# The product with w_spatial as seven products of quarters, whose forms of w_spatial are kept in HBM

## The chip, the core and the metric

The kernel runs on one core of a Trainium2 chip. The metric is device time in microseconds (us), the median of several executions. A core has TensorE (PE in the profile; PEld is its weight load), VectorE (DVE), ScalarE (ACT) and GpSimd (POOL) for the arithmetic, and SyncE (SP), whose queue issues all the DMAs here. Matmuls read their two operands from SBUF and add up in banks of PSUM; the other engines bring results from there back to SBUF.

## What is computed

```python
def _attn_ref(q, k, v, n_global, n_local):          # 4 batches, 8 heads, 768 tokens, head_dim 64
    scores = scale * np.matmul(q, k.transpose(0, 1, 3, 2))
    keep = is_global | is_local                      # 8 global keys, 96 local ones
    scores = np.where(keep, scores + bias, -1000000000.0)
    a = np.exp(scores - max)
    a = a / (sum + 1e-09)
    return np.matmul(a, v)

def _moe_ref(x, w_in, w_spatial, b_spatial, w_out):  # x: [4, 768, 512], w_in: [512, 1024]
    h = np.maximum(x @ w_in, 0.0)
    u, v = (h[..., :d_ff // 2], h[..., d_ff // 2:])
    v_n = (v - mu) / np.sqrt(var + 1e-06)            # mean and variance over the 512 features
    v_s = np.einsum('ts,bsd->btd', w_spatial, v_n) + b_spatial[None, :, None]
    return (u * v_s) @ w_out                         # w_spatial: [768, 768], w_out: [512, 512]
```

The einsum is the product that the change is about: for each batch a 768 x 768 matrix times 768 tokens x 512 features.

## The kernel before

A batch has 768 tokens, six blocks of 128. The program walks through 24 blocks, n = 0 to 23, of attention (scores S, exponentials, transposes, values A), and between them does the pieces of the second function, named by letters in the table `CFG`: V (relu and normalization of one block's v), U (the relu of u for a chunk of 256 tokens), G (the product with w_spatial for a chunk, and the gate), O (the product with w_out, and the result's DMA), and in the first batch the loads: I (w_in), Q (w_out), T (w_spatial), B (b_spatial). The digit behind the letter is the lag in batches, the next the chunk or block: G and O of a batch run while the attention of the next batch does; for the last batch they stand in `END`, with nothing of a next batch beside them.

To keep float32 accuracy, an operand is held as two numbers of TensorE's fast float32 format, a rounded one and the rest (`hi_lo`: a copy that rounds, and a subtraction), and each product is three passes: high by high, high by low, low by high. In `mlp_s` (G) a chunk takes, for each of four blocks of 128 features, 3 passes x 6 blocks of source tokens, that is 18 matmuls of 128x128 by 128x256. Over 3 chunks and 4 batches that is 864 matmuls. The weights' side, `w_t_h` and `w_t_l`, is loaded and split once (`setup_w_t`) and stays in SBUF; the normalized v is split per block into `vnh` and `vnl` (`mlp_v`). Of two accumulated results DVE adds b_spatial (`ev<-bank,b_bc`), DVE or POOL multiplies by u, and `hi_lo` makes `gh` and `gl`, which `mlp_o` multiplies by w_out.

The calls between on and off of the recorder are not issued but recorded, and a planner (`plan`) then sets the order on every engine: it plays the program through with a table of costs (`cost`), waits between engines (`CROSS`) and ranks (`RANKS`, one number for each recorded operation), and picks an engine where an operation may run on several (`any_of`, fixed by `PINS`). PSUM is handed out as six banks by the same planner. `keep_warm` puts matmuls that nobody reads (transposes of the identity, fillers below) into stretches of the start where the planner sees TensorE without work for over 0.9 us. The order is fixed in the program; on the chip every engine works through its own list, and waits where an operand isn't there.

## Time and profile before

| what | value |
|---|---|
| median of 3 runs | 466.04 us (465.19 to 467.04) |
| the profiled execution's own time | 465.66 us |
| its span, first to last instruction | 463.8 us |
| TensorE busy | 449.2 us, 97% |
| VectorE / ScalarE / GpSimd busy | 299.8 / 205.1 / 194.3 us |
| bytes moved by DMA | 35.97 MB, 78 GB/s on the mean |
| granted TensorE clock, mean | 0.992 of full speed |

The busy times say how full an engine is on the mean; what sets the end is in the chain of waits, which follows the last instruction back to what released it, piece by piece. A busy TensorE isn't one at its peak: the time from one matmul's start to the next one's is read from its timeline.

### The profile page before, as it was taken

To read this page: it belongs to the slowest core of one execution; us is meant where nothing else is said; L and a number is where in the kernel's file an instruction comes from. 1 tells how busy PE (TensorE), PEld (TensorE's weight loads), DVE (VectorE), ACT (ScalarE), POOL (GpSimd) and SP (SyncE) were. 2 spreads that over 40 slices of the span, in tenths; PEclk is the share of its full clock that TensorE was granted. 3 is DMA by queue.
4 is the path that set the end of the run, shared out by engine and by line. 5 is a ranking of instruction groups with operands and counts; after the bars stand their busy time and mean duration, and the time that the engine had idled before them with its cause. 6 is when DMAs were issued, how large, how long until landed. Compare 5 with 4: busy or idle time off the path is not lost.

```text
span 463.8 us, 9906 instructions
## 1 busy us (share of the span) xinstructions
PE 449.2 (97%) x3712; PEld 402.2 (87%) x3712; DVE 299.8 (65%) x922; ACT 205.1 (44%) x593; POOL 194.3 (42%) x295
## 2 busy tenths in 40 slices
PE   8579999999999999999999999999999999999996
PEld 8457789899888989899988989899989889899995
DVE  4889998925677899854146898885332577742333
ACT  3877875310448676532012687565011454610001
POOL 2988564334357545221323745365013436211311
PEclk9889999999999999999999999999999999999999
DMA  7876123300213223201012323120002011000012
GB/s 259 309 250 213 61 78 116 116 24 10 105 47 114 98 76 101 92 2 47 1 45 75 114 96 99 52 93 25 1 24 74 24 52 53 7 1 1 23 47 75
DMA packets 17531, 35.97 MB, mean 78 GB/s; under 512 B 2116, under 2 KB 2372, under 8 KB 17476
## 3 DMA queue, kind: packets, MB, share of 16 engines
q1 hardware_dynamic: 17476, 35.27, 23.2%
q8 instruction: 31, 0.51, 0.5%
q14 instruction: 24, 0.20, 0.1%
HBM read 28.97 MB, written 6.29 MB: 76 GB/s over the span
## 4 chain that ended last, share of the span: by engine, by line
PE 90%; DVE 4%; DMA 3%; issue 1%; SPq 0%; POOL 0%; ACT 0%; DVEq 0%
PE bank L49 73%; PE ops L47 8%; PE bank L47 8%; DMA u<-in_moe_w_in_dram 2%; DVE pr L49 1%; DMA vring<-in_v_dram 1%; DVE bank L49 1%; DVE w_in_l L49 1%; SPq L49 0%; POOL pr L49 0%; DVE rawh L49 0%; DVE xtl L49 0%; DVE q L49 0%; DVE rc L49 0%; DVE ev L49 0%
## 5 line engine op out<-in xcount | busy, mean ns | idle before, releaser
L49 ACT ACTIVATE pr<-pr,mn 128x256 f32<-128x256 f32 (+1 forms) x192 | 92.2, 483 | 18.8 <-DVE mn L49 17.2
L49 DVE CUSTOM_DVE_ANT_0 pr<-bank,bias 128x256 f32<-128x256 f32 (+1 forms) x192 | 69.8, 395 | 24.8 <-PE bank L49 14.0
L49 POOL TENSOR_SCALAR pr<-pr,rc 128x256 f32<-128x256 f32 (+1 forms) x115 | 55.5, 495 | 53.6 <-DVE rc L49 26.1
L49 ACT ACTIVATE ev<-bank 128x512 f32<-128x512 f32 (+1 forms) x37 | 21.6, 584 | 97.0 <-PE bank L49 92.0
L49 PE MATMUL bank<-ident,pr 128*128 128x128 f32 x352 | 54.3, 279 | 7.6 <-POOL pr L49 5.9
L49 DVE TENSOR_TENSOR ev<-bank,b_bc 128x512 f32<-128x512 f32 x24 | 16.6, 690 | 59.4 <-PE bank L49 54.0
L49 PEld LDWEIGHTS bank<-ident,pr 128*128 128x128 f32 x352 | 40.9, 142 | 15.5 <-POOL pr L49 6.9
L49 ACT ACTIVATE pth<-bank 128x512 f32<-128x512 f32 (+1 forms) x67 | 36.2, 560 | 37.2 <-PE bank L49 33.7
L47 PE MATMUL ops<-pth,vring 128*64 128x128 f32 x704 | 44.5, 279 | 0.0
L47 PE MATMUL bank<-kring,q 64*128 64x256 f32 (+1 forms) x528 | 43.6, 307 | 0.7 <-DVE mn L49 0.7
L49 PE MATMUL bank<-w_t_l,vnh 128*128 128x256 f32 x288 | 44.2, 282 | 0.0
L47 PEld LDWEIGHTS ops<-pth,vring 128*64 128x64 f32 x704 | 38.7, 139 | 5.7 <-issue 4.3
L49 PE MATMUL bank<-w_t_h,vnh 128*128 128x256 f32 x288 | 42.9, 282 | 0.0
L49 PE MATMUL bank<-w_t_h,vnl 128*128 128x256 f32 x288 | 42.8, 282 | 0.0
L47 PEld LDWEIGHTS bank<-kring,q 64*128 64x128 f32 x528 | 35.0, 188 | 8.2 <-issue 3.7
L49 POOL TENSOR_TENSOR gl<-ev,gh 128x512 fp32r<-128x512 f32 x14 | 18.1, 1293 | 53.3 <-PE bank L49 34.7
L49 PEld LDWEIGHTS bank<-w_t_l,vnh 128*128 128x128 f32 x288 | 39.0, 189 | 0.7
L49 PEld LDWEIGHTS bank<-w_t_h,vnh 128*128 128x128 f32 x288 | 38.1, 189 | 0.5 <-issue 0.2
L49 PEld LDWEIGHTS bank<-w_t_h,vnl 128*128 128x128 f32 x288 | 38.0, 189 | 0.5 <-issue 0.2
L49 ACT ACTIVATION_READ_ACCUMULATOR pr<-pr,mn 128x1 f32 x192 | 36.4, 189 | 0.0
L49 PE MATMUL bank<-xth,w_in_l 128*128 128x256 f32 x192 | 33.7, 287 | 0.0
L49 DVE TENSOR_SCALAR pr<-pr,rc 128x256 f32<-128x256 f32 (+1 forms) x77 | 32.2, 443 | 0.5
(133 smaller groups left out, 870.9 us busy)
## 6 DMA issues: line engine op xcount, KB each, us to landing
vring<-in_v_dram SPq DMA_DIRECT2D x24, 256.0 KB, 2.8
out_dram<-ev SPq DMA_DIRECT2D x23, 256.0 KB, 2.0
u<-in_moe_w_in_dram SPq DMA_DIRECT2D x8, 512.0 KB, 5.1
rawh<-in_q_dram SPq DMA_DIRECT2D x9, 256.0 KB, 2.5
raw<-in_q_dram SPq DMA_DIRECT2D x9, 256.0 KB, 2.7
raw<-in_k_dram SPq DMA_DIRECT2D x9, 256.0 KB, 2.6
rawh<-in_k_dram SPq DMA_DIRECT2D x9, 256.0 KB, 2.8
kring<-in_k_dram SPq DMA_DIRECT2D x6, 256.0 KB, 5.0
```

Source lines behind the costliest of these rows:

```text
L47: self.real.matmul(**{n: placed(x) for n, x in kw.items()})
L49: getattr(self.real, self.call)(*[placed(x) for x in self.args], **{n: placed(x) for n, x in self.kw.items()})
```

## The change

The 768 x 768 matrix is cut into four quarters of 384 x 384, and v into four quarters of 384 tokens x 256 features (even or odd token blocks, lower or upper features). The result's quarters are then built from seven products of quarters, where a plain product takes eight. Each product takes sums or differences of quarters on both sides:

- `setup_w_t` makes the seven forms of w_spatial (four additions of 384 columns per pair of token blocks), `put_t` splits each with `hi_lo` and stores it to HBM: 3 pairs x 7 forms, 21 stores of 393 KB. Before, six blocks were split into SBUF.
- `mlp_s` (G, now seven steps per batch, in the order 0, 1, 4, 3, 6, 5, 2) loads one form, 1.18 MB, into one of two buffers `wts`: 28 loads, 33.0 MB. It makes v's side (`sx`, four additions of 128x768 per batch), splits it (`oper`), and does 2 x 9 matmuls of 128x128 by 128x384: 126 per batch, 504 in all. Each of the two results is added from PSUM by DVE (`ga`, `gt`, `gx`, each 128x384), joined with others in SBUF, and multiplied into u in place (`gate`).
- `mlp_v` no longer splits v; it stays whole for the batch (`vr`, one buffer). u is one tile for the batch (one buffer). `mlp_o` (O, six steps of 128 tokens) splits the gated u into `gg` right before its matmuls; their number and shape stay.
- The tables `RANKS` and `PINS` are new, and the entries of `CFG`: T moves from the first three to the fourth to sixth block of the first batch, Q into the second batch (`T1`). w_in's loads take the same slots as before (three parts of the tile `u`); the path for wide masks follows the new `mlp_s` and `mlp_o`, and isn't run with these inputs.

```diff
@@ -25,11 +25,12 @@
...
 CFG = {
     "WS": 6, "conv": "pp", "SG": 4, "SG0": 2, "WG": 4, "kept": "p", "bias1": "x", "bias2": "x", "whi": "x", "wth": "x", "wtl": "x",
-    "qhi": "x", "qlo": "x", "khi": "x", "klo": "x", "pth": "x", "xh": "x", "xl": "v", "vnh": "x", "vnl": "x",
+    "qhi": "x", "qlo": "x", "khi": "x", "klo": "x", "pth": "x", "xh": "x", "xl": "v", "wts": "x", "oph": "x", "opl": "x", "ops": "x", "gk": "x", "b_ga": 2, "b_gd": 2, "b_gt": 2, "b_gx": 3, "b_gx2": 2, "b_oper": 2, "b_wts": 2,
     "gm": "x", "gh": "x", "gl": "x", "o": "vava", "norm0": "x", "norm": "x", "vrn": "v", "b_ev": 3, "b_pr": 10, "b_pth": 4,
-    "S": [["I01", "A"], ["I00", "T00", "T01", "A", "V00", "B00"], ["T02", "T03", "A", "V01", "U00"], ["T04", "T05", "A", "V02"], ["Q00", "Q01", "A", "V03", "U01"], ["Q02", "Q03", "A", "V04"]],
-    "T": [["V15", "U12", "A"], ["G10", "O10", "A"], ["G11", "O11", "A"], ["G12", "O12", "V00", "V01", "U00", "A"], ["V02", "A"], ["V03", "U01", "A", "V04"]],
-    "END": ["V05", "U02", "G00", "O00", "G01", "O01", "G02", "O02"],
+    "S": [["I01", "A"], ["I00", "A", "V00", "B00"], ["A", "V01", "U00"], ["T00", "A", "V02"], ["T01", "A", "V03", "U01"], ["T02", "A", "V04"]],
+    "T1": [["V15", "U12", "A"], ["Q00", "Q01", "G10", "G11", "G12", "A"], ["Q02", "Q03", "G13", "G14", "G15", "A"], ["G16", "O10", "O11", "V00", "V01", "U00", "A"], ["O12", "O13", "V02", "A"], ["V03", "O14", "O15", "U01", "A", "V04"]],
+    "T": [["V15", "U12", "A"], ["G10", "G11", "G12", "A"], ["G13", "G14", "G15", "A"], ["G16", "O10", "O11", "V00", "V01", "U00", "A"], ["O12", "O13", "V02", "A"], ["V03", "O14", "O15", "U01", "A", "V04"]],
+    "END": ["V05", "U02", "G00", "G01", "G02", "G03", "G04", "G05", "O03", "G06", "O04", "O05", "O00", "O01", "O02"],
 }
 NLMAX = 97
...
-WORDS = {"gh": 1024, "gl": 1024, "pth": 512, "vring": 1536, "kring": 2048, "pr": 256, "s": 512, "p": 512, "m": 512, "ops": 1024, "q0": 1024, "q1": 1024}
-BUFS = {"gh": 1, "gl": 1, "u": 3, "s": 2, "p": 2, "m": 2, "raw0": 1, "raw1": 1, "rawh0": 1, "rawh1": 1}
+WORDS = {"gg": 1024, "oper": 1536, "u": 3072, "wts": 2304, "gx2": 768, "pth": 512, "vring": 1536, "kring": 2048, "pr": 256, "s": 512, "p": 512, "m": 512, "ops": 1024, "q0": 1024, "q1": 1024}
+BUFS = {"u": 1, "gg": 2, "s": 2, "p": 2, "m": 2, "raw0": 1, "raw1": 1, "rawh0": 1, "rawh1": 1}
...
 RANKS = [
-    -1227.13, -1206.24, -272.31, -662.83, 46.11, -326.88, -663.12, -104.90, -322.98, 496.15, -312.43, -1165.63, -37.37, -80.04, -1204.73, -1162.10,
+    -410.76, -386.18, -131.71, -256.51, -115.72, -216.04, -217.17, -54.52, -50.49, 10.95, -223.60, -450.53, -4.15, -17.85, 95.48, 0.39,
...
@@ -961,9 +950,11 @@
...
-    w_t_h = const.tile([P, NB, S], F32R, name="w_t_h")
-    w_t_l = const.tile([P, NB, S], F32R, name="w_t_l")
+    HS = S // 2
+    parked = {}
     b_bc = const.tile([P, S], F32, name="b_bc")
+    b_two = const.tile([P, HS], F32, name="b_two")
+    dram = ctx.enter_context(tc.tile_pool(name="dram", bufs=1, space=bass.MemoryType.DRAM))
...
@@ -1098,15 +1097,38 @@
...
     def setup_w_t(b, t):
-        st = work.tile([P, S], F32, name="wst3", tag=("gh", "gl")[t % 2], bufs=1)
-        nc.sync.dma_start(out=st, in_=w_sp[t * P:(t + 1) * P, :])
-        hi_lo(st, w_t_h[:, t], w_t_l[:, t], E("wth", t), E("wtl", t))
+
+        st = [work.tile([P, S], F32, name="wst3", tag="gg", bufs=2) for _ in range(2)]
+        for x in range(2):
+            nc.sync.dma_start(out=st[x], in_=w_sp[(2 * t + x) * P:(2 * t + x + 1) * P, :])
+        b11, b12, b21, b22 = (st[x][:, y * HS:(y + 1) * HS] for x in range(2) for y in range(2))
+        d1, d2 = (work.tile([P, HS], F32, name="wd", tag="ev", bufs=nb("ev")) for _ in range(2))
+        e = E("wts")
+        put_t(0, t, b11)
+        two(e, d1, b12, b11, ALU.subtract)
+        put_t(3, t, d1)
+        two(e, d1, b22, d1, ALU.subtract)
+        put_t(4, t, d1)
+        put_t(1, t, b21)
+        two(e, d1, b21, d1, ALU.subtract)
+        put_t(6, t, d1)
+        two(e, d2, b22, b12, ALU.subtract)
+        put_t(5, t, d2)
+        put_t(2, t, b22)
+
+    def put_t(x, t, src):
+        if x not in parked:
+            parked[x] = dram.tile([P, 2, NB // 2, HS], F32, name=f"w_t{x}")
+        pair = work.tile([P, 2, HS], F32R, name="wtp", tag="gx2", bufs=nb("gx2"))
+        hi_lo(src, pair[:, 0], pair[:, 1], E("wth", t), E("wtl", t))
+        nc.sync.dma_start(out=parked[x][:, :, t], in_=pair.bitcast(F32))
...
     def setup_b(b, j):
         nc.sync.dma_start(out=b_bc, in_=b_sp.partition_broadcast(P))
+        two(None, b_two, b_bc[:, HS:], b_bc[:, 0:HS], ALU.subtract)
...
@@ -1289,7 +1311,9 @@
...
         for x, (a, w, t) in enumerate(passes):
...
-        vr = work.tile([P, FH], F32, name="vr", tag="ev", bufs=nb("ev"))
+        if i == 0:
+            vn[b] = work.tile([P, NB, FH], F32, name="vr", bufs=1)
+        vr = vn[b][:, i]
         nc.scalar.activation(vr, ps, AF.Relu)
...
@@ -1305,12 +1329,12 @@
...
         else:
...
-        t = vn[b, i] = tuple(work.tile([P, FH], F32R, name=f"vn{x}", bufs=6) for x in "hl")
-        hi_lo(vr, t[0], t[1], E("vnh"), E("vnl"))
...
     def mlp_u(b, c):
         xh, xl = xt[b, c]
-        u = uu[b, c] = work.tile([P, NF, CH], F32, name="u", bufs=3)
+        if c == 0:
+            uu[b] = work.tile([P, NF, S], F32, name="u", bufs=1)
+        u = uu[b]
         for fp in range(NF // 2):
             if nc.open:
                 nc.token((b, "U", c, fp), nc.now[1])
@@ -1320,45 +1344,105 @@
...
                 for x, (w, a, t) in enumerate(passes):
...
-            nc.scalar.activation(u[:, 2 * fp:2 * fp + 2], ps, AF.Relu)
-
...
+            nc.scalar.activation(u[:, 2 * fp:2 * fp + 2, c * CH:(c + 1) * CH], ps, AF.Relu)
+
+    ORDER = (0, 1, 4, 3, 6, 5, 2)
+    TIMES_OF = {0: 0, 1: 1, 4: 4, 3: 3, 6: 2, 5: 5, 2: 6}
+    form = {}
+
+    def mlp_s(b, y):
+
+        vr, u = vn[b], uu[b]
+        NH = NB // 2
+        a11, a12, a21, a22 = (vr[:, x::2, y_ * CH:(y_ + 1) * CH] for y_ in range(2) for x in range(2))
+        tok = nc.now
+        e = E("ops")
+        x = ORDER[y]
+
+        def temp():
+            return work.tile([P, NH, CH], F32, name="sx", tag="sx", bufs=2)
+
+        def side(tag):
+            return work.tile([P, HS], F32, name=tag, tag=tag, bufs=nb(tag))
+
+        def gate(j, half, other, by):
+            part = u[:, 2 * half + j, other * HS:(other + 1) * HS]
+            two(E("gm"), part, by, part, ALU.mult)
+
+        if nc.open:
+            nc.token((b, "G", y, 0), tok[1])
+        if x == 0:
+            src = a11
+        elif x == 1:
+            src = a12
+        elif x == 2:
+            src = a22
+        elif x == 4:
+            form[0], form[1] = temp(), temp()
+            two(e, form[0], a21, a22, ALU.add)
+            two(e, form[1], form[0], a11, ALU.subtract)
+            src = form[1]
+        elif x == 3:
+            src = form[0]
+        elif x == 6:
+            two(e, form[1], a12, form[1], ALU.subtract)
+            src = form[1]
+        else:
+            two(e, form[0], a11, a21, ALU.subtract)
+            src = form[0]
+        w = work.tile([P, 2, NH, HS], F32R, name="wts", tag="wts", bufs=nb("wts"))
+        nc.sync.dma_start(out=w.bitcast(F32), in_=parked[TIMES_OF[x]])
+        hl = work.tile([P, 2, NH, CH], F32R, name="oper", tag="oper", bufs=nb("oper"))
+        hi_lo(src, hl[:, 0], hl[:, 1], E("oph"), E("opl"))
+        b1 = b_bc[:, HS:]
+        add = nc.vector.tensor_tensor
+        for j in range(2):
             if nc.open:
...
+                nc.token((b, "G", y, 1 + j), tok[1])
+            ps = ps_m.tile([P, HS], F32, name="sps", tag="m")
+            for i, (m, z, p) in enumerate((m, z, p) for m, z in ((0, 0), (0, 1), (1, 0)) for p in range(NH)):
+                nc.tensor.matmul(ps, lhsT=hl[:, m, p, j * P:(j + 1) * P], rhs=w[:, z, p], start=(i == 0), stop=(i == 3 * NH - 1))
+            if x == 0:
+                form["a", j] = side("ga")
+                add(out=form["a", j], in0=ps, in1=b1, op=ALU.add)
+            elif x == 1:
+                g = side("gx")
+                add(out=g, in0=ps, in1=b_two, op=ALU.subtract)
+                two(E("gm"), g, form["a", j], g, ALU.add)
+                gate(j, 0, 0, g)
+            elif x in (4, 5):
+                add(out=form["a", j], in0=ps, in1=form["a", j], op=ALU.add)
+                if x == 5:
+                    two(E("gm"), form["d", j], form["d", j], form["a", j], ALU.add)
+                    gate(j, 1, 1, form["d", j])
+            elif x == 3:
+                form["d", j] = side("gd")
+                cp(E("gk"), form["d", j], ps)
+                form["t", j] = side("gt")
+                two(E("gm"), form["t", j], form["a", j], form["d", j], ALU.add)
+            elif x == 6:
+                add(out=form["t", j], in0=ps, in1=form["t", j], op=ALU.add)
+                gate(j, 0, 1, form["t", j])
+            else:
+                g = side("gx")
+                add(out=g, in0=ps, in1=b_two, op=ALU.subtract)
+                two(E("gm"), g, form["a", j], g, ALU.add)
+                gate(j, 1, 0, g)
+
+    def mlp_o(b, i):
+        last = (b, i) == (B - 1, NB // 2 - 1)
+        ga = work.tile([P, 2, NF, P], F32R, name="gg", tag="gg", bufs=2)
+        hi_lo(uu[b][:, :, i * P:(i + 1) * P], ga[:, 0], ga[:, 1], E("gh", i), E("gl", i))
+        ps = ps_m.tile([P, DM], F32, name="ops2", tag="m")
+        passes = [(x, w, f) for fp in range(0, NF, 2) for x, w in ((0, w_out_h), (0, w_out_l), (1, w_out_h)) for f in (fp, fp + 1)]
+        o = work.tile([P, DM], F32, name="o", tag="ev", bufs=nb("ev"))
+        half = DM // 2 if last else DM
+        for lo in range(0, DM, half):
+            cs = slice(lo, lo + half)
+            for y, (x, w, f) in enumerate(passes):
+                nc.tensor.matmul(ps[:, cs], lhsT=ga[:, x, f], rhs=w[:, f, cs], start=(y == 0), stop=(y == len(passes) - 1))
+            cp(E("o", i), o[:, cs], ps[:, cs])
+            nc.sync.dma_start(out=out[b, i * P:(i + 1) * P, cs], in_=o[:, cs])
...
@@ -1385,7 +1469,7 @@
     for n in range(B * NB):
         b, i = divmod(n, NB)
         more = n + 1 < B * NB
-        for tok in CFG["S" if b == 0 else "T"][i]:
+        for tok in CFG["S" if b == 0 else "T1" if b == 1 else "T"][i]:
             if tok == "A":
...
                     nc.token(("P", n + 1), n + .2)
...
```

What the tables make of it at three places, read from the programs' instruction lists.

TensorE, last batch, before: the products with w_spatial beside those with w_out. `w_t_h` and `w_t_l` are the matrix in SBUF, `vnh` and `vnl` blocks of v, `gh` the gated result, `bank` a PSUM bank.

```order
L49 MATMUL bank_89<-w_t_l,vnh_140 128x256
L49 MATMUL bank_89<-w_t_l,vnh_147 128x256
L49 MATMUL bank_90<-w_out_h,gh_162 128x512 x2
L49 MATMUL bank_90<-w_out_l,gh_162 128x512
L49 MATMUL bank_89<-w_t_l,vnh_149 128x256
L49 MATMUL bank_89<-w_t_l,vnh_151 128x256
L49 MATMUL bank_89<-w_t_l,vnh_157 128x256
L49 MATMUL bank_89<-w_t_l,vnh_159 128x256
```

TensorE, last batch, now: from the end of the third product (buffer `wts_163`) over matmuls of U (`xth`, `xtl` with `w_in`) to the end of the fourth (`wts_159`); the row that follows is the fifth product's first, from `wts_163` again.

```order
L50 MATMUL bank_95<-wts_163,oper_164 128x384 x4
L50 MATMUL bank_90<-xtl_139,w_in_h 128x256 x2
L50 MATMUL bank_90<-xth_138,w_in_l 128x256 x4
L50 MATMUL bank_90<-xth_138,w_in_h 128x256 x4
L50 MATMUL bank_90<-xtl_139,w_in_h 128x256 x4
L50 MATMUL bank_90<-xth_138,w_in_l 128x256 x4
L50 MATMUL bank_93<-xth_138,w_in_h 128x256 x4
L50 MATMUL bank_93<-xtl_139,w_in_h 128x256 x3
L50 MATMUL bank_91<-wts_159,oper_160 128x384
L50 MATMUL bank_95<-wts_159,oper_160 128x384 x7
L50 MATMUL bank_91<-wts_159,oper_160 128x384 x8
L50 MATMUL bank_95<-wts_159,oper_160 128x384 x2
```

Between two uses of one buffer there are now 25 matmuls of U and the other buffer's 18; before, U was done with earlier, and nothing was loaded here.

SP's queue, last batch, before: keys' and values' last loads (`vring`), then results (`out_dram`).

```order
L49 DMA vring_119<-in_v_dram 32x512
L49 DMA vring_119<-in_v_dram 128x512
L49 DMA out_dram<-ev_108 128x512
L49 DMA vring_119<-in_v_dram 128x512
L49 DMA vring_119<-in_v_dram 32x512 x2
L49 DMA out_dram<-ev_108 128x512
L49 DMA out_dram<-ev_106 128x512 x2
L49 DMA out_dram<-ev_107 128x512
```

SP's queue, last batch, now: `w_t_<number>` are the forms in HBM.

```order
L50 DMA out_dram<-ev_109 128x512
L50 DMA vring_120<-in_v_dram 32x512
L50 DMA wts_163<-w_t_149 128x2304
L50 DMA wts_159<-w_t_147 128x2304
L50 DMA wts_163<-w_t_153 128x2304
L50 DMA wts_159<-w_t_152 128x2304
L50 DMA wts_163<-w_t_151 128x2304
L50 DMA out_dram<-ev_107 128x512
```

Five loads of 1.18 MB now stand between the last values and the last results; each waits for the matmuls that free its buffer. The first two forms of the batch are loaded ahead of these rows.

SP's queue, second batch's attention (where the first batch's G begins), before: w_out's last load between loads for the attention.

```order
L49 DMA vring_119<-in_v_dram 128x512 x2
L49 DMA raw_0_121<-in_k_dram 128x512
L49 DMA gl_136<-in_moe_w_out_dram 128x1024
L49 DMA raw_0_121<-in_k_dram 128x512
L49 DMA rawh_0_123<-in_k_dram 128x512
L49 DMA out_dram<-ev_108 128x512
```

SP's queue, the same place now: `gx_0` and `gx_1` are the two buffers that `put_t` stores from.

```order
L50 DMA vring_120<-in_v_dram 128x512 x2
L50 DMA w_t_145<-gx_0_146 256x1x384
L50 DMA gg_143<-in_moe_w_out_dram 128x1024
L50 DMA w_t_147<-gx_1_148 256x1x384
L50 DMA wts_159<-w_t_145 128x2304
L50 DMA w_t_149<-gx_0_146 256x1x384
L50 DMA w_t_150<-gx_1_148 256x1x384
L50 DMA gg_143<-in_moe_w_out_dram 128x1024
L50 DMA raw_0_122<-in_k_dram 128x512
L50 DMA wts_163<-w_t_150 128x2304
L50 DMA w_t_151<-gx_0_146 256x1x384
L50 DMA wts_159<-w_t_149 128x2304
```

The last stores of the forms, w_out's loads and the first loads of the forms now stand in one stretch, and a load waits for the store of its form's third part.

## Rows read from the trace of the kernel before

**Rows 1.** The page: busy us (share of the span) and instructions of each engine.

```profile
PE 449.2 (97%) x3712; PEld 402.2 (87%) x3712; DVE 299.8 (65%) x922; ACT 205.1 (44%) x593; POOL 194.3 (42%) x295
```

**Rows 2.** The page: GB/s moved by DMA in 40 equal slices of the span.

```profile
GB/s 259 309 250 213 61 78 116 116 24 10 105 47 114 98 76 101 92 2 47 1 45 75 114 96 99 52 93 25 1 24 74 24 52 53 7 1 1 23 47 75
```

**Rows 3.** The chain of waits in order of time: start us, us, what.

```profile
47.95 0.31 DVE pr L49
...
48.32 1.14 PE bank L47 x8
...
407.35 52.19 PE bank L49 x365
459.54 0.02 issue
459.56 0.38 ACT ev L49
```

**Rows 4.** PE, groups: form xcount | busy us, mean ns | idle before.

```profile
L49 PE MATMUL bank<-w_t_l,vnh 128*128 128x256 f32 x288 | 44.2, 282 | 0.0
...
L49 PE MATMUL bank<-ident 128*128 128x128 f32 x98 | 13.6, 302 | 1.7 <-POOL ident masks.py:199 1.7
```

**Rows 5.** PE, timeline of the last batch: start us, us, operation, how many.

```profile
427.12 1.58 PE L49 MATMUL bank<-w_t_h,vnh 128*128 128x256 f32 x12
428.54 1.10 PE L49 MATMUL bank<-w_t_l,vnh 128*128 128x256 f32 x8
...
450.99 0.62 PE L49 MATMUL bank<-w_out_h,gh 128*128 128x512 f32 x2
...
453.78 0.40 PE L49 MATMUL bank<-w_out_h,gh 128*128 128x256 f32 x2
```

**Rows 6.** PE, timeline of the start.

```profile
7.66 3.93 PE L49 MATMUL bank<-ident 128*128 128x128 f32 x34
11.52 1.16 PE L47 MATMUL bank<-kring,q 64*128 64x128 f32 x16
...
20.25 2.34 PE L49 MATMUL bank<-ident,pr 128*128 128x128 f32 x8 [5.15 <-POOL pr L49]
...
51.29 1.09 PE L49 MATMUL bank<-ident,pr 128*128 128x128 f32 x8
```

**Rows 7.** Windows: busy us by engine, granted TensorE clock, DMA share, GB/s.

```profile
20.00:25.00 5.00, 4.70 (x20) 2.95 (x22) 4.06 (x12) 2.64 (x8) 3.78 (x7) 0.50 0.39 129
25.00:30.00 5.00, 4.21 (x39) 3.40 (x36) 4.19 (x21) 4.49 (x15) 4.42 (x8) 0.89 0.92 281
...
76.00:77.00 1.00, 1.00 (x11) 1.00 (x10) 0.32 (x1) 0.55 (x1) 0.90 (x2) 1.00 1.01 373
77.00:78.00 1.00, 1.00 (x11) 1.00 (x10) 1.00 (x4) 0.35 (x2) 0.00 (x0) 1.00 0.98 340
```

**Rows 8.** DMA issues: xcount, KB each, median us from issue to landing.

```profile
vring<-in_v_dram SPq DMA_DIRECT2D x24, 256.0 KB, 2.8
...
u<-in_moe_w_in_dram SPq DMA_DIRECT2D x8, 512.0 KB, 5.1
...
gh<-in_moe_w_out_dram SPq DMA_DIRECT2D x2, 512.0 KB, 3.4
```

**Rows 9.** Other engines, groups by shape, as in rows 4.

```profile
L49 DVE TENSOR_TENSOR ev<-bank,b_bc 128x512 f32<-128x512 f32 x24 | 16.6, 690 | 59.4 <-PE bank L49 54.0 <-POOL gl L49 3.1 <-DMA out_dram<-ev 2.1
...
L49 POOL TENSOR_TENSOR gl<-ev,gh 128x512 fp32r<-128x512 f32 x14 | 18.1, 1293 | 53.3 <-PE bank L49 34.7 <-ACT gh L49 9.6 <-DVE gh L49 8.1
...
L49 POOL TENSOR_TENSOR w_t_l<-gh,w_t_h 128x768 fp32r<-128x768 f32 x3 | 5.5, 1847 | 0.1
...
L49 DVE TENSOR_TENSOR gl<-ev,gh 128x512 fp32r<-128x512 f32 x10 | 6.9, 689 | 4.9 <-POOL gh L49 4.1 <-ACT gh L49 0.5
...
L49 DVE TENSOR_TENSOR q<-rawh,q 128x512 fp32r<-128x512 f32 x5 | 4.6, 921 | 0.0
...
L49 DVE TENSOR_TENSOR w_t_l<-gl,w_t_h 128x768 fp32r<-128x768 f32 x1 | 0.9, 927 | 0.0
```

More of the change, by code (lines that the diff above doesn't have):

```diff
@@ L1048, in scaled, with load_weights @@
             nc.gpsimd.tensor_scalar(out=out, in0=in_, scalar1=by, scalar2=1.0, op0=ALU.mult, op1=ALU.mult)
-    def load_weights(src, tag):
-        st = work.tile([P, src.shape[-1], 2], I32, name="wst", tag=tag)
+    stage = []
+    def load_weights(src, tag, x):
+        w = src.shape[-1]
+        if tag == "u":
+            if not stage:
+                stage.append(work.tile([P, NF * S], F32, name="wst", tag=tag, bufs=1))
+            st = stage[0][:, (x % 3) * 2 * w:(x % 3 + 1) * 2 * w].bitcast(I32).rearrange("p (w two) -> p w two", two=2)
+        else:
+            st = work.tile([P, w, 2], I32, name="wst", tag=tag, bufs=2)
         nc.sync.dma_start(out=st.rearrange("p w two -> p (w two)"), in_=src.bitcast(I32))
@@ L1346, in mlp_o @@
-    def mlp_o(b, c):
-        gh, gl = gated[b, c]
-        last = (b, c) == (B - 1, NCH - 1)
-        for x in range(CH // P):
-            if nc.open:
-                nc.token((b, "O", c, x), nc.now[1])
-            ps = ps_m.tile([P, DM], F32, name="ops2", tag="m")
-            passes = [(a, w, f) for fp in range(0, NF, 2) for a, w in ((gh, w_out_h), (gh, w_out_l), (gl, w_out_h)) for f in (fp, fp + 1)]
-            o = work.tile([P, DM], F32, name="o", tag="ev", bufs=nb("ev"))
-            half = DM // 2 if last and x == CH // P - 1 else DM
-            for lo in range(0, DM, half):
-                cs = slice(lo, lo + half)
-                for y, (a, w, f) in enumerate(passes):
-                    nc.tensor.matmul(ps[:, cs], lhsT=a[:, f, x * P:(x + 1) * P], rhs=w[:, f, cs], start=(y == 0), stop=(y == len(passes) - 1))
-                cp(E("o", x), o[:, cs], ps[:, cs])
-                nc.sync.dma_start(out=out[b, c * CH + x * P:c * CH + (x + 1) * P, cs], in_=o[:, cs])
+            nc.scalar.activation(u[:, 2 * fp:2 * fp + 2, c * CH:(c + 1) * CH], ps, AF.Relu)
```

109 lines of the change are left out of this document (46 added, 63 removed), and 487 rows, old and new, of the table RANKS.

## The prediction, made before the changed kernel was run

> **What bounds the kernel now.** I read the engines' busy times first: TensorE is busy for 449.2 of 463.8 us, VectorE for 299.8, the others for less than half the span [rows 1]. Then the chain of waits, since a mean doesn't say what ends last: up to 48.3 us it runs through DMAs and VectorE, from there through TensorE, up to the last result's copy by ScalarE at 459.56 [rows 3]; its last piece alone is 52.19 us of matmuls without a break. So what leaves TensorE's list after the first 50 us leaves the time, provided that nothing new makes TensorE wait. How long a matmul occupies TensorE is read from starts, not from the mean of one (282 ns in [rows 4], which overlap): twelve of 256 columns take 428.54 - 427.12 = 1.42 us, 118.3 ns each; twelve of 512 take 453.78 - 450.99 = 2.79 us, 232.5 ns each [rows 5].
>
> **TensorE's own list.** Gone are 864 matmuls of 256 columns (three groups of 288 [rows 4]): 864 x 118.3 ns = 102.2 us. New are 504 of 384 columns, a width that the trace doesn't show. Scaled from the 256-wide ones it takes 177.5 ns, from the 512-wide ones 174.4, and in the middle between the two 175.4, which I take, since the two differ by a fixed part per matmul: 88.4 us. That is **-13.8 us**, with ends at -12.7 and -14.3. All other matmuls stay (by the lists, V 288, U 576, O 300, and attention's), as do the changes between attention's small matmuls and the others (92 against 89).
>
> **The loads.** Each product needs 1.18 MB from HBM in one of two buffers, freed by the product two before it. If the load is late, TensorE stands. In the last batch nothing of a next one fills in: between the third product's end and the fifth's start stand 25 matmuls of U and 18 of the fourth product, 25 x 0.118 + 18 x 0.175 = 6.1 us. Counted in the same way, the gaps of the last batch are 6.2, 6.1, 6.1, 6.1 and 6.1 us, and of the first three batches 10.4, 9.4, 8.1, 6.2, 7.6; 8.1, 6.2, 8.5, 6.5, 6.3; 6.7, 6.8, 7.1, 7.1, 7.2. Against this the load: 256 KB land after 2.8 us and 512 KB after 3.4, on a quiet queue [rows 8], so 0.6 us per 256 KB; the 1152 KB of a form would land after 3.4 + 2.5 x 0.6 = 4.9 us. While one DMA has the engines for itself it moves 340 to 373 GB/s [rows 7], so 1.18 MB need 3.2 to 3.5 us, beside 512 KB's 1.4 to 1.5, and land after 5.1 to 5.5. With an allowance of 0.3 us for the handoffs from TensorE to the queue and back (no row shows them alone), 5.2 to 5.8 us pass between a buffer's release and its next use: just under 6.1. I put these waits at **0**, at most +3. The start's 512 KB loads, among many others, took 5.1 us [rows 8]; at that rate a form takes 11 us, which is the first rival below.
>
> The Trainium skill (DMA: Bandwidth & Descriptors, "Anatomy of one DMA") gives some 2.0 us of fixed cost plus bytes over 436 GB/s. For 512 KB that makes 3.2 us, where the trace has 3.4; for a form it makes 4.7, and the waits would be 0 by it too, with 1 us to spare instead of 0.3 to 0.9.
>
> **The first batch's traffic.** There the forms are made, stored and read back. From the first product to the last of that batch are about 43 us of TensorE; in that stretch SP's list has 6 of the 21 stores (2.4 MB), seven loads of forms (8.3 MB), three of w_out (1.6 MB) and attention's (about 1 MB): 13 MB, or 310 GB/s, as much as the fullest slice of the trace of before has, and that is at the start (309 [rows 2]), where the chain does run through DMAs. In-order on SP, a store that waits for its `hi_lo` also holds back the form behind it. Attention and U give this stretch's gaps up to 10 us. I take **+2 us**, 0 to +6: the lower end if all is hidden, the upper if three of the five loads are late by two stores' time (0.4 MB each at 350 GB/s, 1.1 us).
>
> **The start.** Before 48 us TensorE waits and runs 98 fillers (13.6 us with their overlap [rows 4]); after 5.15 us of idling its clock is granted at 0.50 from 20 to 25 us, which is the lower level, 1.2 GHz, and eight transposes take 2.34 us instead of 1.09 [rows 6, 7]. Now the first scores' q and k are at the head of SP's list and stand behind 42 fillers instead of 67, then 55 and 28 fillers bridge the stretch up to the first transposes, which start at about the same time (33 + 9 + 55 + 28 against 33 + 34 + 11 fillers and 5.15 us of idling), but at the full clock. VectorE is what bounds the next 25 us, and it idled for only 1.75 us between 20 and 30 [rows 7]; its list up to the fourth block's scores has about the same work, since w_spatial was split mostly on the other engines. **-1 us**, from -3 to +2 (the first form's work is early in VectorE's list, and the 83 fillers delay real work if it is ready sooner).
>
> **The other engines.** VectorE gets 48 additions of 384 columns from PSUM for 24 of 512 (690 ns, so about 555 for 384), 25 operations of 128x768 on two operands in SBUF (927) and some 68 smaller ones (0.55 to 0.69), and loses 63 of 512 (0.43 to 0.74): together with copies and more normalizations that it takes over from POOL, about +53 us, to 353 of 453, 78%. POOL gets 19 operations of 128x768 (1847 ns) and 45 of 384 (about 1.0 us), loses 33 additions or products of 512 at 1.29 and 14 copies: +16, to 210. ScalarE +20, to 225. None is the bound on the mean [rows 1, 9]; the cover is TensorE's own list, and without it VectorE's 53 us would be the price. In the last batch the first and second product need v's last two blocks: after V's last matmul come ScalarE, two steps of VectorE, two of POOL, one of VectorE and the rounding, seven operations of at most 0.9 us, with their handoffs an estimated 4.6 us; 5.3 us of matmuls stand in between. **0**, at most +2.
>
> **The end.** The last product's result passes three steps of VectorE before the split and the last three O; 7.5 us of O of other tokens stand in between. The last copy and its DMA stay as they are: 4.3 us of span behind the last matmul, and 1.9 us outside the span. **0**.
>
> **Sum**, against the profiled execution's 465.66 us, 0.4 under the median of the three runs: 465.7 - 13.8 + 0 + 2 - 1 = 452.9; on the scale of the median **453.2 us**.
>
> **Rivals.** *The loads come late, and it is slower.* The place is the 20 gaps above. A wait at one product lengthens the next one's gap, so about every second one counts. With 8 us from release to use the waits add up to 1.8 + 3.5 + 3.0 + 5.6 = 13.9 us, which is all of the gain; with 9 us to 23, and the time is 476. For it: the 5.1 us of the start's 512 KB loads, and a queue that must also fetch for attention. Against it: the middle of the run moves 1 to 116 GB/s [rows 2], and in the last batch the five loads follow each other on SP with nothing between. The point is 7.9 us. Chance 0.08 for slower than 468.4.
> *Late in the first batch only, or by a little everywhere (6.5 to 7.5 us):* 3 to 9 us are lost, 457 to 463.5. Chance 0.14.
> *VectorE and POOL hold each other up.* POOL's long operations beside VectorE's: a subtraction of 128x512 on VectorE took 689 ns in one group and 921 in another, beside POOL's 1.29 us [rows 9], so 0.23 us per operation in bad company. In the last batch's 31 us of products, VectorE has 8 operations of 768 and 6 of 384 on two operands in SBUF, POOL 3 and 6: 7.4 + 3.3 + 5.5 + 6.1 = 22 us if no two ever ran together, so 9 are to spare; 0.23 more on each still leaves 4. If it decides in the batches before, where attention's work is added, I price it at 0.23 x 200 operations = 46 us of VectorE, which then stands at 88%, and a fifth of that on TensorE: 462, within the band "same" or just under. Chance 0.06.
> The Trainium skill (SBUF — State Buffer, on the port pair that VectorE and GpSimd share) has such operations exclude each other for their whole length; the 921 against 689 agrees that they can delay each other, and the 22 of 31 us is the sum by that rule.
> *The change doesn't do what it says:* a 384-wide matmul at 200 ns or more would eat the saving, 465 to 468. Nothing between 118 for 256 and 232 for 512 suggests it; with other ways to end there 0.03.
> *More than forecast:* the start gains 4 us or more, or nothing is lost in the first batch; under 449. Chance 0.07.
> The forecast, 449 to 457: 0.62.
>
> **Numbers.** Range 448.5 to 462, which leaves out the slow rival, the two near 465 and half of those under 449. Beyond 0.5% (463.7 to 468.4 is the band that a measurement can't tell from no change): faster 0.62 + 0.14 + 0.07 + half of 0.06 = 0.86, which I lower to 0.84 for what I don't see in so many new instructions; same 0.06; slower 0.10.
>
> **What the profile after would show.** TensorE busy near 435 us; a group of 504 matmuls with `wts`, with starts 175 ns apart; from about 50 us on a chain through TensorE alone, and no wait of TensorE for `wts`' DMA in the last batch beyond 0.3 us each; loads of 1152 KB landing after 4.9 to 5.5 us; VectorE near 350 us. I am wrong if TensorE's idle time lists the DMA of `wts` or the engines that make `oper` for more than a few us, if loads land after 7 us or more, or if the first 50 us grow.

## The result: 461.0 us against 465.9, and where the forecast gain went

The changed kernel takes 460.96 us (median of 11 executions, 457.25 to 464.03) against 465.89 (11, 465.19 to 467.83): 0.988 of the time before, with a 95% interval from 0.985 to 0.991. That is 4.9 us faster, clear of the noise; 12.8 were forecast. The profiled execution took 461.96 us and its span is 460.0, 3.8 us shorter than the kernel before's 463.8.

The page of the changed kernel: busy us of the engines and GB/s by slice (as [rows 1, 2]), then the new group of products (columns as in [rows 4]).

```profile
PE 442.0 (96%) x3379; PEld 393.4 (86%) x3379; DVE 358.2 (78%) x1014; ACT 229.1 (50%) x634; POOL 223.2 (49%) x301
...
GB/s 252 336 169 157 208 239 222 230 297 243 344 230 159 222 138 136 79 76 143 216 178 103 226 138 162 43 131 23 250 291 107 155 70 75 7 104 213 199 53 92
...
L50 PE MATMUL bank<-wts,oper 128*128 128x384 f32 x504 | 104.1, 349 | 5.2 <-DMA wts<-w_t 4.5
```

TensorE's list is shorter as forecast. In the last batch's timeline (start us, us, operation, how many) 18 matmuls of 384 columns take 408.56 - 405.39 = 3.17 us, 176 ns each:

```profile
405.39 3.33 PE L50 MATMUL bank<-wts,oper 128*128 128x384 f32 x18
408.56 0.40 PE L50 MATMUL bank<-xth,w_in_h 128*128 128x256 f32 x2
```

504 x 176 ns = 88.7 us stand for 102.2, so the list lost 13.5 us, and 3.8 arrived in the span. The group's last column says what stood in between: TensorE idled 4.5 us for the DMA of `wts`. The chain of waits (start us, us, what) has both places, in the first batch:

```profile
88.17 3.92 DMA w_t<-gx
...
92.15 8.37 DMA wts<-w_t
...
100.57 10.48 PE bank L50 x54
...
129.81 8.57 DMA wts<-w_t
...
138.52 6.64 PE bank L50 x34
```

The third part of the first form is stored from 88.17 to 92.09; its load goes at 92.15 and needs 8.37 us. The sixth product's load, issued as its buffer comes free at 129.81, needs 8.57. Over the whole run a form lands after 5.4 us (DMA issues: KB each, median us from issue to landing; answers to [rows 8]):

```profile
wts<-w_t SPq DMA_DIRECT2D x28, 1152.0 KB, 5.4
w_t<-gx SPq DMA_DIRECT2D x21, 384.0 KB, 3.8
...
gg<-in_moe_w_out_dram SPq DMA_DIRECT2D x4, 512.0 KB, 6.0
```

Windows around the two waits (columns as in [rows 7]; the last three are the granted clock, the DMA engines' share and GB/s):

```profile
95.00:100.00 5.00, 3.65 (x36) 3.11 (x34) 4.72 (x13) 1.85 (x5) 3.88 (x8) 1.00 0.86 311
100.00:105.00 5.00, 4.43 (x17) 4.43 (x18) 1.99 (x5) 1.66 (x4) 1.11 (x2) 0.67 0.85 244
...
130.00:135.00 5.00, 5.00 (x37) 5.00 (x35) 5.00 (x11) 2.46 (x5) 2.21 (x3) 1.00 0.81 291
135.00:140.00 5.00, 2.46 (x16) 2.29 (x15) 3.17 (x7) 0.60 (x1) 4.03 (x3) 0.93 0.84 315
140.00:145.00 5.00, 5.00 (x30) 4.90 (x28) 2.69 (x5) 1.32 (x3) 0.00 (x0) 0.73 0.11 30
```

Up to the end of each wait the DMA engines are busy for 81 to 86% of the time at 244 to 315 GB/s, and after each wait the granted clock falls to 0.50, the lower level of 1.2 GHz (from 102 to 104 and from 140 to 142 us), so that the next window stands at 0.67 and 0.73. From 150 us on TensorE is busy without a break up to its last matmul; no later load makes it wait. Behind that matmul stand 6.5 us of span instead of 4.3 (the expectations below have 6.4, and 2.1 us for the difference; the timelines give 2.2).

### The profile page after: what moved, and what is told of

Same layout as the page of the kernel before. It is cut to its first block, busy times and chain, and to the rows that moved or that the text cites. A ratio compares the mean times of both kernels' runs of the same rounds, so it can differ in the third digit from the quotient of the medians.

```text
span 460.0 us, 9501 instructions
## 1 busy us (share of the span) xinstructions
PE 442.0 (96%) x3379; PEld 393.4 (86%) x3379; DVE 358.2 (78%) x1014; ACT 229.1 (50%) x634; POOL 223.2 (49%) x301
## 4 chain that ended last, share of the span: by engine, by line
PE 82%; DMA 8%; DVE 4%; ACT 1%; SPq 1%; POOL 1%; issue 1%; DVEq 0%; POOLq 0%
PE bank L50 67%; PE ops L48 8%; PE bank L48 7%; DMA wts<-w_t 4%; DMA w_t<-gx 2%; DMA u<-in_moe_w_in_dram 2%; DVE pr L50 1%; SPq L50 1%; DVE bank L50 1%; ACT pth L50 0%; DVE ev L50 0%; POOL pr L50 0%; ACT pr L50 0%; DVE pth L50 0%; DVE q L50 0%
## 5 line engine op out<-in xcount | busy, mean ns | idle before, releaser
L50 PE MATMUL bank<-wts,oper 128*128 128x384 f32 x504 | 104.1, 349 | 5.2 <-DMA wts<-w_t 4.5
L50 PEld LDWEIGHTS bank<-wts,oper 128*128 128x128 f32 x504 | 88.8, 193 | 8.0 <-DVE vr L50 2.7
L50 POOL TENSOR_SCALAR pr<-pr,rc 128x256 f32<-128x256 f32 (+1 forms) x97 | 48.4, 511 | 56.3 <-DVE rc L50 48.0
L50 PE MATMUL bank<-w_out_h,gg 128*128 128x512 f32 (+1 forms) x200 | 56.5, 390 | 0.0
L50 PEld LDWEIGHTS bank<-w_out_h,gg 128*128 128x128 f32 x200 | 36.0, 188 | 7.2 <-DVE gg L50 0.3
L50 PE MATMUL bank<-xtl,w_in_h 128*128 128x256 f32 x192 | 34.6, 286 | 0.0
L50 PE MATMUL bank<-xth,w_in_h 128*128 128x256 f32 x192 | 33.4, 287 | 0.0
L50 PE MATMUL bank<-w_out_l,gg 128*128 128x512 f32 (+1 forms) x100 | 31.1, 386 | 0.0
L50 PE MATMUL bank<-w_in_h,xth 128*128 128x512 f32 x96 | 28.6, 406 | 1.2 <-DVE mn L50 1.0
L50 PEld LDWEIGHTS bank<-xth,w_in_l 128*128 128x128 f32 x192 | 28.2, 190 | 0.5 <-issue 0.2
```

The costliest lines, as they stand in the source:

```text
L50: getattr(self.real, self.call)(*[placed(x) for x in self.args], **{n: placed(x) for n, x in self.kw.items()})
```

## Experiments

All times are medians; beside each the ratio to the kernel before and its interval. The changed kernel itself was run again beside three of them:

> The changed kernel itself, beside the others on the same chip: 459 to 462 us, and a spread of 3 us or more between its runs, as before.

460.00 us (five executions, 456.52 to 463.28). Over all 16 executions its median is 460.5, from 456.5 to 464.0; what follows is compared with that.

### Loads taken away

All 28 loads cut to 192 KB, at the moment of issue:

```diff
+        if self.call == "dma_start" and kw["out"].tensor.name.startswith("wts"):
+            kw = {n: x[:, 0, 0] for n, x in kw.items()}
```

> The changed kernel, with each of the 28 loads of a form cut from 1152 KB to 192 KB (three of its six blocks of 128x384 are not loaded at all, and every product's matmuls read the one block that is; the instructions of all engines and their order stay). Theory A (the lost time is the first batch's loads, which land after 8.4 to 8.6 us, 2.1 and 2.5 us of TensorE's waits, and the lower clock after them, 1.7 us each): no wait for a form, the clock at 1.00 from 55 us on, 451 to 454 us. Rival B (the lost time is in TensorE's own list, or on other engines): no wait for a form either, but 457 us or more.

456.28 us (0.979, 0.976 to 0.983). The products' timeline; in brackets the idle time before and what ended it:

```profile
98.83 2.42 PE L55 MATMUL bank<-wts,oper 128*128 128x384 f32 x13
...
107.38 3.40 PE L55 MATMUL bank<-wts,oper 128*128 128x384 f32 x18
...
133.59 2.55 PE L55 MATMUL bank<-wts,oper 128*128 128x384 f32 x13 [1.99 <-DVE gt L55]
...
139.78 1.56 PE L55 MATMUL bank<-wts,oper 128*128 128x384 f32 x8
```

The first product starts without a wait, the clock stays up. The sixth still waits 2 us, now for VectorE's `gt`. So 4.2 us come back, between the two theories' bands (451 to 454, 457 or more): theory A has the right place, but the loads hid a second limit (the section on VectorE and GpSimd), and what is lost behind the last matmul stays.

With only the first batch's seven loads small:

```diff
+        if FIRST[0] and self.call == "dma_start" and kw["out"].tensor.name.startswith("wts"):
+            FIRST[0] -= 1
```

> The changed kernel, with only the first batch's seven loads cut to 192 KB (the other five blocks of 128x384 not loaded, the batch's matmuls read the one block); the 21 loads of the later batches stay whole. Theory A (only the first batch's loads cost anything): as with all 28 small, 455.5 to 457 us, and no wait for a form later on. Rival G (all loads cost a little, by contention in HBM or SBUF): half-way, 458 to 459 us.

457.32 us (0.981, 0.980 to 0.983), 1.0 us from the run with all small; TensorE waited 0.4 us in all for a form. The 21 later loads cost that 1 us at most; with overlapping intervals it may be nothing.

### What makes them late

18 of the 21 stores cut to a twenty-fourth:

```diff
+        if ... kw["in_"].tensor.name.startswith("gx2") and not kw["out"].tensor.name.startswith("w_t0"):
+            kw = {n: x[:, :, 0:16] for n, x in kw.items()}
+        if ... kw["out"].tensor.name.startswith("wts"):
+            kw["in_"] = FROM[0]
```

> The changed kernel, with 18 of the 21 stores of the forms cut from 384 columns to 16 (the three of the first form stay whole, and every load reads that form, so six of the seven products of each batch are taken with the wrong form; all instructions and their order stay). Theory A1 (what makes the first batch's loads late is what the DMA engines have to move at the same time): 3 MB less in the stretch from 88 to 137 us, the loads there land after 5.4 to 6.5 us instead of 8.4 to 8.6, the waits for them shrink to under 1 us, 455 to 457.5 us, as with the small loads. Rival A2 (the first load is late because it is issued late, behind the third store of its own form, and TensorE's wait follows from that): the first load still goes at 92 us and the first product still waits by 1 to 2 us, 459 to 461 us.

457.43 us (0.983, 0.979 to 0.987). That is in A1's band. The first load went at 91.16, 1 us earlier, and had landed when the first product began at 98.48 without a wait, so within 7.3 us instead of 8.4; all waits for a form made 0.9 us. A2 falls as the whole account: the issue moved by 1 us, the landing by at least 2. But this run doesn't part the traffic from a second thing that it takes away. A load waits for the store of its own form to land, and that wait shrinks with the stores: in the changed kernel SyncE's queue waited for stores twice from 85 to 150 us (3.0 us in all), here not at all, and the second load went at 100.22 instead of 102.56.

w_out's four loads cut to 128 KB:

```diff
+        if ... kw["in_"].tensor.name.startswith("in_moe_w_out"):
+            kw = {n: x[:, 768:1024] for n, x in kw.items()}
```

> The changed kernel, with the four loads of w_out cut from 512 KB to 128 KB (three quarters of w_out are not loaded; what stands in the staging buffer is converted instead). 1.5 MB less in the stretch from 89 to 130 us. Theory A1: each late load comes about 1 us sooner, TensorE waits 2 to 3 us instead of 5, 457.5 to 459.5 us. Rival A2: no change, 460 to 462 us.

455.22 us (0.976, 0.973 to 0.980), more than A1 expected. The waits for a form fell to 1.3 us, and here the stores are whole. The wait for `gt` was gone too, and that isn't the loads: VectorE stands still for w_out between 88 and 150 us neither here nor in the changed kernel, but GpSimd's operation on 128x768 began at 131.25, when VectorE's two normalizations (130.68 to 131.28) were done; the section on VectorE and GpSimd shows what it costs when they meet. So 2.3 MB of stores less (six of 384 KB lose 23 of 24 parts each; the 3 MB of the expectation are too many) or 1.6 MB of w_out less are each enough, which fits what is moved between 88 and 137 us as the bound. That the total counts, and not what stands ahead of each load on the queue, isn't shown.

### The clock

Transposes of the identity in the two waits:

```diff
+    FILL = {(0, 0): 18, (0, 5): 22}
+        warm[x:x] = [filler(bank) for _ in range(many)]
```

> The changed kernel, with 18 transposes of the identity (2.0 us) put ahead of the first product and 22 (2.5 us) ahead of the sixth, where TensorE waits for a load. Theory A: the loads land when they did, TensorE's clock stays at 1.00 through both waits, and 1.7 us are won after each: 457 to 459 us. Rival D (the clock costs nothing, since TensorE is held up by something else there anyway): 460 to 462 us.

462.60 us (0.992, 0.988 to 0.995): nothing won, and just above D's band. The 2 us over the changed kernel lie within overlapping intervals. First the changed kernel's timeline:

```profile
98.37 0.28 PE L50 MATMUL bank<-xtl,w_in_h 128*128 128x256 f32 x1
100.57 3.57 PE L50 MATMUL bank<-wts,oper 128*128 128x384 f32 x13 [1.92 <-DMA wts<-w_t]
...
111.81 3.36 PE L50 MATMUL bank<-wts,oper 128*128 128x384 f32 x18 [0.77 <-DVE pth L50]
...
138.52 3.85 PE L50 MATMUL bank<-wts,oper 128*128 128x384 f32 x13 [2.54 <-DMA wts<-w_t]
...
146.25 1.58 PE L50 MATMUL bank<-wts,oper 128*128 128x384 f32 x8
```

then with the transposes:

```profile
98.77 2.13 PE L50 MATMUL bank<-ident 128*128 128x128 f32 x18
100.70 2.54 PE L50 MATMUL bank<-wts,oper 128*128 128x384 f32 x13
...
111.72 4.93 PE L50 MATMUL bank<-wts,oper 128*128 128x384 f32 x18 [2.11 <-DMA wts<-w_t]
...
140.01 2.50 PE L50 MATMUL bank<-wts,oper 128*128 128x384 f32 x13
...
146.17 1.58 PE L50 MATMUL bank<-wts,oper 128*128 128x384 f32 x8
```

The clock stayed at 1.00 through the first wait, and the first product took 13 matmuls in 2.5 us instead of 3.6. But the second product's load lands at 111.7 anyway. It did in the changed kernel too (issued at 102.56, 9.1 us), where the second product began at 111.81; the profile names VectorE's `pth` there, which was done 0.1 us after the load. Up to there the loads set the time, and TensorE's slower clock was covered: D is right. What was saved became a wait of 2.1 us ahead of the second product, the granted clock fell there instead (0.50 from 114 to 116 us), and its 18 matmuls took 4.9 us instead of 3.4. At the sixth product theory A is right: it began 1.5 us later, but 13 matmuls took 2.5 us instead of 3.85, and both executions begin its last eight at 146.2. So the transposes moved the idle time and the lower clock by one product; that the clock costs nothing isn't what they show.

### Loads in halves

Two DMAs of 576 KB for one of 1152:

```diff
+            for z in range(2):
+                self.real.dma_start(out=kw["out"][:, z], in_=kw["in_"][:, z])
```

First with the matmuls put in another order:

> The changed kernel, with each load of a form issued as two DMAs of 576 KB, upper halves first, and each product's matmuls put so that those on the upper half come first (for the very first product both column halves' upper parts ahead of the lower ones). Theory A: the first product needs its second half only 2.1 us after it began, the sixth 1.05 us, so the two waits fall from 4.6 to about 1.5 us, the clock stays up at least once: 454 to 458 us. Rival B: the time stays at 460 to 462 us. Rival C (twice the DMAs on one queue cost more than they give): over 462 us.

465.87 us (0.998, 0.997 to 1.000), 5 us slower than the changed kernel: in C's band, but not for C's reason. What TensorE waited for (us in total, times, longest):

```profile
PE bank L55 <- ACT oper L55: 5.9, 6, 1.0
PE bank L55 <- DMA wts<-w_t: 2.2, 1, 2.2
...
PE bank L55 <- POOL oper L55: 1.4, 2, 0.9
...
PE bank L55 <- DVE oper L55: 0.6, 1, 0.6
```

The waits for loads were halved, but the new order needs the lower part of the other operand 0.5 us sooner, and 7.9 us went there. So the halves alone:

> The changed kernel, with each load of a form issued as two DMAs of 576 KB, upper halves first; the matmuls stay in their order, in which the lower half is needed 0.5 us after the upper. If what cost 5 us in the run with split loads and moved matmuls was the moving (TensorE then waited 7.9 us for the engines that make the lower part of the other operand), this gives 459.5 to 461.5 us, no more than 1 us better than the changed kernel; if it was the 28 additional DMAs on the queue, 463 us or more.

456.42 us (0.980, 0.977 to 0.983), better than I expected: 4 us under the changed kernel, with nothing left out.

```profile
98.23 1.04 PE L55 MATMUL bank<-wts,oper 128*128 128x384 f32 x5
99.51 1.69 PE L55 MATMUL bank<-wts,oper 128*128 128x384 f32 x8 [0.24 <-DMA wts<-w_t]
...
133.80 3.34 PE L55 MATMUL bank<-wts,oper 128*128 128x384 f32 x13 [2.14 <-DVE gt L55]
```

The first product begins on the upper half at 98.23 and waits 0.24 us for the lower. The sixth waits for `gt`, as with the small loads.

> The changed kernel, with the two DMAs of 576 KB for the first batch's seven loads alone; the 21 later loads stay whole. Theory A (what the split wins, it wins in the first batch): 456 to 457.5 us, as with all split. Rival: the split wins in the later batches too, by an earlier release: 458.5 to 460 us.

457.94 us (0.982, 0.981 to 0.984), between the two bands: 2.5 of the 3 to 4 us are won in the first batch. 0.7 to 1.1 us of the rest aren't won by loads at all: behind the last matmul 6.3 us of span are left here, and 5.6 and 5.2 in the two profiled executions with all loads in halves (see "The end").

### w_out's loads behind

```diff
+        y = next(y for y in range(x, len(warm)) if ... warm[y].writes[0].tensor.name.startswith("wts"))
+            warm.insert(y, warm.pop(x))
```

> The changed kernel, with each of w_out's four loads put on SyncE's queue behind the next load of a form instead of ahead of one; nothing else moves. Theory A1 (shared DMA engines): the first, second and sixth load of a form no longer share with the 512 KB issued 1.4 to 3.5 us before them, land up to 1.4 us sooner (512 KB at 350 GB/s), and two of TensorE's waits shrink by about 1 us each: 457.5 to 460 us. Rival H (w_out's split, now later, holds up the engines that make it, and they TensorE): 461 us or more.

> Both edits on the changed kernel: the loads of the forms as two DMAs of 576 KB, and w_out's loads behind them. With the split alone it took 456.4 us and TensorE's last wait for a form was 0.2 us; what was left there was 2.1 us for VectorE's sum ahead of the sixth product. If the loads are no longer the bound, moving w_out's gives nothing more: 455.5 to 457 us. If they still are: 454 to 455 us. If w_out's split comes too late: over 458 us.

472.43 us (1.014, 1.012 to 1.016) and, with the halves, 471.67 (1.012, 1.011 to 1.014): H, 12 us over the changed kernel; its band was open upwards. VectorE's waits in the first of the two, from 88 to 150 us:

```profile
DVE raw L50 <- DMA gg<-in_moe_w_out_dram: 6.1, 2, 5.1
DVE ev L50 <- DMA gg<-in_moe_w_out_dram: 5.9, 1, 5.9
DVE rawh L50 <- DMA gg<-in_moe_w_out_dram: 3.1, 1, 3.1
```

w_out's split stands in VectorE's fixed row ahead of the products' sums and attention's work. It stood 15 us for w_out, and TensorE behind it (11 us for results of VectorE in three waits).

### VectorE and GpSimd

The halves again, then with one operation of GpSimd given to VectorE:

> The changed kernel with every load of a form as two DMAs of 576 KB, once more and with more runs, as the reference for the next two: 455.5 to 457.5 us.

> The split loads, and one instruction moved: in the first batch the lower half of the seventh product's other operand (128x768) is made by VectorE, behind the two sums that the sixth product waits for, instead of by GpSimd beside them. Theory J (an operation of GpSimd on operands in SBUF holds VectorE's next one up to its own end: 2.04 us where it takes 0.41, and that is TensorE's last wait of 2.1 us in the first batch): the wait falls under 0.6 us and the clock stays up behind it, 453 to 455 us. Rival K (VectorE is simply full there): VectorE has 0.9 us more to do, the wait stays at 2 us, 456 to 458 us.

```diff
+        if op.eng == "gpsimd" and op.token[0] == (0, "G", 6, 0) and op.writes[0].tensor.name.startswith("oper"):
+            op.take(next(w for w, way in enumerate(op.ways) if way[0].name == "vector"))
```

457.31 us (0.980, 0.978 to 0.982) and 455.83 (0.978, 0.974 to 0.981; six executions from 453.80 to 463.31, 455.44 without the longest). The timelines around the sixth product, first of the halves alone (GpSimd, VectorE, TensorE):

```profile
133.19 2.10 POOL L55 TENSOR_TENSOR oper<-vr,oper 128x768 fp32r<-128x768 f32 x1 [0.97 <-ACT oper L55]
...
133.49 2.21 DVE L55 TENSOR_SCALAR pr<-pr,rc 128x256 f32<-128x256 f32 x2
...
136.69 3.53 PE L55 MATMUL bank<-wts,oper 128*128 128x384 f32 x11 [1.99 <-DVE gt L55]
...
144.42 1.56 PE L55 MATMUL bank<-wts,oper 128*128 128x384 f32 x8
```

then with the operation moved (VectorE, TensorE):

```profile
133.20 0.61 DVE L55 TENSOR_SCALAR pr<-pr,rc 128x256 f32<-128x256 f32 x2
...
134.79 0.79 PE L55 MATMUL bank<-wts,oper 128*128 128x384 f32 x3
...
135.89 2.01 PE L55 MATMUL bank<-wts,oper 128*128 128x384 f32 x10 [0.31 <-DMA wts<-w_t]
...
141.54 1.56 PE L55 MATMUL bank<-wts,oper 128*128 128x384 f32 x8
```

Two normalizations on VectorE take 2.21 us while GpSimd works on 128x768 from 133.19 to 135.29; without GpSimd beside them they take 0.61. TensorE's wait for `gt` is gone and the clock of this execution is 1.00 throughout. That is J's mechanism. Up to the fifth product's last fifteen matmuls (129.91 and 129.89 us) the two executions agree to 0.1 us; the sixth product's last eight begin 2.9 us apart, for the wait and the clock behind it. The Trainium skill (SBUF — State Buffer, "SBUF: two separate sides") describes the port pair of the two as a lock held for the whole operation, and this trace agrees: VectorE's pair ends at 135.70, 0.4 us after GpSimd's operation. In the medians it is 1.5 us, with overlapping intervals, and the time lies between J's band and K's; so the wait is shown, and what it is worth in the median isn't. Of the kernels here that leave nothing out it has the lowest median, 2.2% under the kernel before.

### The end

Code that these inputs don't run, cut to a quarter:

```diff
     def general():
-            for b in range(B):
+            for b in range(1):
```

> The changed kernel, with the code behind the flag at its end (which these inputs do not run) cut from four batches to one. Theory E (the end is 2.1 us longer since SyncE's jump over that code takes 3.1 us instead of 0.4): the last matmul ends 4.3 us before the span instead of 6.4, 458.5 to 459.5 us. Rival F (the end is longer because the last copy is VectorE's, or for the last DMA): 460 to 462 us.

458.06 us (0.983, 0.979 to 0.987). SyncE's instructions at the flag (count, duration ns, first and last start us) in the kernel before, the changed one, and this:

```profile
L1505 SPq EVENT_SEMAPHORE  x8: 17/17/17, 461.4 to 462.3; - x8
...
L1505 SPq COMPARE_BRANCH  x1: 50/50/50, 460.9 to 460.9; - x1
```

```profile
L1590 SPq EVENT_SEMAPHORE  x8: 17/17/17, 458.1 to 458.6; - x8
...
L1590 SPq COMPARE_BRANCH  x1: 45/45/45, 455.0 to 455.0; - x1
```

```profile
L1590 SPq EVENT_SEMAPHORE  x8: 17/17/17, 453.7 to 454.9; - x8
...
L1590 SPq COMPARE_BRANCH  x1: 45/45/45, 453.2 to 453.2; - x1
```

From the branch to the next instruction pass 0.5, 3.1 and 0.5 us; the last matmul ends 4.3, 6.5 and 4.8 us before the span does. So the cut brings back 1.6 us of the 2.2. Most of the rest is VectorE's own jump: the last copy is VectorE's now, and its jump takes 2.9 us, where ScalarE's, behind the last copy of the kernel before, took 2.5. The other 1.8 us of this execution's shorter span lie in the first batch (the sixth product's last eight matmuls begin at 144.43 instead of 146.25), which the cut doesn't touch; the median's gain isn't the end's alone.

> The split loads, and the code behind the flag (not run on these inputs) cut from four batches to one. Theory E (SyncE's jump over it costs the changed kernel 1.3 to 2 us at the end): with the split loads SyncE's jump already took 0.6 us in the profiled run, so little is left to win: 455.5 to 457 us. Rival L (the cut itself saves 2 to 3 us in any kernel, by the other engines' jumps): 453 to 454.5 us.

> The kernel before, with the same cut of the code behind the flag. Theory E: its SyncE jumps in 0.4 us as it is, so the cut wins at most 0.5 us: 465.3 to 466 us. Rival L: 463 to 464 us.

455.90 us (0.979, 0.977 to 0.982), 1.4 under the halves alone, within their spread; and 465.86 (1.000, 0.999 to 1.002) for the kernel before: the cut saves nothing there, so L falls. With the halves SyncE jumped in 0.5 us although its unused code is the same. It goes with the program: in the nine traces with the later loads whole and the code uncut SyncE takes 2.7 to 3.1 us, in the five with all loads in halves 0.5 to 0.6. What in the program decides stays open.

## Why the forecast was half wrong

The sum, term by term, for the profiled executions: list -13.5, first batch's traffic +6.6, VectorE behind GpSimd +2.0, end +2.2, and -1.1 left for everything else, together -3.8.

- **TensorE's list, -13.8:** right, -13.5 at 176 ns.
- **The loads, 0:** right outside the first batch. The 20 loads issued after 150 us land after 5.0 to 7.2 us, 5.2 in the median (4.9 to 5.5 said), and no product waits for one. [rows 7] was misread on the way: at 76 to 78 us two 256 KB loads and one of 512 KB share the 340 to 373 GB/s. A form that lands alone moves 415 (411 to 413 us of the changed kernel), so the estimate came out right all the same. The Trainium skill's 4.7 us (DMA: Bandwidth & Descriptors, "Anatomy of one DMA") is an estimate by a fit for DMAs that GpSimd issues, and these are SyncE's; it was 0.3 us under the fastest landing.
- **The first batch's traffic, +2 (0 to +6): the step that failed.** The traffic and its 310 GB/s were seen; their effect was mis-sized. Between the first product's readiness (98.65 in the changed kernel, 98.83 with small loads) and the second's start (111.81 and 107.38) 4.6 us are lost, and by the sixth product's last eight matmuls (146.25 and 139.78) 6.6; both timelines stand above. I let up to three loads be late by two stores' time; in fact the first, the second (covered by the slow clock) and the sixth were late by 2 to 3 us each, with landings of 8.4 us and more instead of 5.5. Left out was the clock behind a wait (13 matmuls at 1.2 GHz took 3.85 us instead of 2.55), though [rows 6, 7] show one. My own sign of being wrong, loads that land after 7 us or more, showed in this batch.
- **The start, -1:** not separated; -1.1 is what the other terms leave over. Its step on the clock was right: over the first 50 us 1.00 was granted, against 0.93 before.
- **Other engines, 0 (at most +2): failed by 2.0.** On the mean it held: VectorE is busy 358.2 us (about 350 said), and its additions of 384 columns took 551 ns (555 said). But TensorE still waits 2.0 us for `gt` with the small loads, by the third rival's mechanism, and 1.5 us in the changed kernel's second profiled execution. The rival was priced by a mean: of the five subtractions of 921 ns in [rows 9] the median is 0.69 us and one took 1.67, so there too a single operation was held up, and not each by 0.23 us.
- **The end, 0: failed by 2.2.** I took the span behind the last matmul as fixed, and never asked what it is made of.
- **Rivals.** "Late in the first batch only", 457 to 463.5 us, is what came; I gave it 0.14. It deserved more, since the only stretch of [rows 2] at 309 GB/s was one in which the chain did run through DMAs. Part of the hit is luck: without the end and VectorE's wait, neither of which it names, the time would have been near 457.

The profile that I announced: TensorE busy 442 instead of 435 (27 more fillers are 3.1 us of it, and matmuls at the lower clock count longer), starts 176 ns apart, a chain through TensorE from 150 instead of 50 us on.

Three things stay open: the wider spread of the changed kernel, the start's share, and what sets SyncE's jump. As to the first, three profiled executions of the same main program had the first product wait 1.92, 2.93 and 1.12 us and the sixth 2.54 (load), 1.50 (`gt`) and 3.03 (load): they meet the same waits differently each time.

## What to carry to other kernels

Price a load at the rate of the stretch in which it is issued, with all that the stretch must move, and let the consumer begin on half a load: two DMAs for one gave back 2.5 us here in the first batch alone, without a byte less to move. Before a transfer is moved out of the way, look who stands in line for what it brings: w_out's loads, one place later, cost 12 us. When a wait is taken away, the next one behind it decides (here VectorE held up by GpSimd), so the gain is read from the run, not from the length of the wait.
